# Two query chunks per step in a thresholded attention followed by a gated MLP: score tiles in pairs, one threshold pass of 2304 columns

## The chip, the cores and the metric

The kernel runs on one core of a Trainium2 chip. The metric is the device time of one execution in microseconds, lower is better. Executions of one kernel agree to about 1% here. Each kernel below was profiled once and, beside the kernel before on the same chip, timed in three rounds.

Engine names in the profile: PE is TensorE (matmuls), PEld its weight loads, DVE VectorE, ACT ScalarE, POOL GpSimd, SPq the queue of the sync engine, which issues nearly all transfers here. L490 is line 490 of the kernel that was profiled, so the same instruction has other line numbers in other kernels.

## The reference, cut to what matters

```python
def _attn_ref(q, k, v, tau):                      # 8 batches, 8 heads, 576 queries, 64 wide
    scores = (1.0 / np.sqrt(64)) * np.matmul(q, k.transpose(0, 1, 3, 2))
    thresh = np.max(scores, axis=-1, keepdims=True) - tau
    scores = np.where(scores >= thresh, scores, -1000000000.0)
    scores = scores - np.max(scores, axis=-1, keepdims=True)
    attn = np.exp(scores)
    attn = attn / (np.sum(attn, axis=-1, keepdims=True) + 1e-09)
    return np.matmul(attn, v)

def _moe_ref(x, w_in, w_spatial, b_spatial, w_out):  # x: 8 x 576 x 512, the heads side by side
    h = np.maximum(x @ w_in, 0.0)
    u, v = h[..., :512], h[..., 512:]
    v_n = (v - mean(v)) / np.sqrt(var(v) + 1e-06)    # over the last axis
    v_s = np.einsum('ts,bsd->btd', w_spatial, v_n) + b_spatial[None, :, None]
    return (u * v_s) @ w_out
```

## The kernel before

The 64 heads are worked on in 32 pairs. The work on one pair is called a slot. The 576 queries are four chunks of 128 for each of the two heads, and one chunk (the remainder) that holds the last 64 queries of both. So a slot has five steps, c = 0 to 4. In a step the kernel

1. multiplies queries with keys into one of two score tiles in PSUM (TensorE),
2. takes each row's maximum (VectorE, `negm`),
3. takes the exponential of scores less maximum (ScalarE, `e`),
4. one step later zeroes what lies under exp(-tau): the threshold pass (VectorE, `p`),
5. after every second chunk transposes both chunks' probabilities by a transfer (`pT`); the remainder's are transposed by a transfer of their own (`ptr<-pr`).

A slot later the transposed probabilities are multiplied with the values: `pv` part 0 (chunks 0 and 1) and part 1 (chunks 2, 3 and the remainder). Beside that, up to two jobs fill each step: transpositions of the next pair's queries and keys on TensorE, the parts of `pv`, and one matmul of the gMLP of the batch before. Each job has a matmul and an eviction from one of two small PSUM banks. The step of the kernel before, cut:

```python
def step(i, c, f1, f2):                 # f1, f2: (engine of the eviction, matmul, eviction)
    if i is not None:
        s = scores(i, c)                                        # PE, one of two score tiles
    while held:
        held.pop(0)()                                           # eviction left by the step before
    if f1:
        f1[1]()
        if f1[0] == "act":
            f1[2]()
    ...
    nc.vector.tensor_reduce(out=nm[:, 0:nh], in_=s, axis=AX.X, op=ALU.max, negate=True)
    if f1 and f1[0] == "dve":
        f1[2]()
    ...                                                         # exponentials on ACT
    if unmasked:
        mask()                                                  # pass over the chunk before
    for f in ready:
        f()                                                     # transfers: outputs, xT
    ...
    if f2:
        f2[1]()
        ...                                                     # its eviction, or held

def mask():
    i, c, e = unmasked.pop()
    if c < 4:
        pt = p_ring[c // 2]
        ef = e.rearrange("p h s -> p (h s)")
        nc.vector.scalar_tensor_tensor(out=pt[:, c % 2, :], in0=ef, scalar=ctau, in1=ef,
                                       op0=ALU.is_ge, op1=ALU.mult)
        if c % 2:
            dst = ptp.tile([P, 2, 9, P], BF16, name="pT")
            nc.sync.dma_start_transpose(...)                    # both chunks
    else:
        pts[i, 2] = ptr_ring[i % 3]
        nc.sync.dma_start_transpose(out=pts[i, 2][:, :, 0:P], in_=pr_ring[i % 2])
```

The order of the jobs in a slot: queries' transposition (c = 0), keys' (c = 1), the remainder's of both (c = 2), `pv` part 0 (c = 3), part 1 (c = 4), each with a gMLP job. GpSimd copies the remainder's keys and queries into block diagonals (`kd`, `qd`) that the scores of the next slot need.

Of the kernel before, what the change touches and what calls it, by code (L numbers as in the profile page):

```python
# [8 lines left out]
F32 = mybir.dt.float32  # L9
BF16 = mybir.dt.bfloat16  # L10
AX = mybir.AxisListType
ALU = mybir.AluOpType
ACT = mybir.ActivationFunctionType
# [4 lines left out]
def kernel(  # L18
# [24 lines left out]
    const = ctx.enter_context(tc.tile_pool(name="const", bufs=1))  # L43
    qkn = ctx.enter_context(tc.tile_pool(name="qkn", bufs=2))
    qkT = ctx.enter_context(tc.tile_pool(name="qkT", bufs=2))
    ep = ctx.enter_context(tc.tile_pool(name="ep", bufs=3))
    ptp = ctx.enter_context(tc.tile_pool(name="ptp", bufs=5))
    small = ctx.enter_context(tc.tile_pool(name="small", bufs=6))
    xp = ctx.enter_context(tc.tile_pool(name="xp", bufs=2))
# [79 lines left out]
    def view(t, off, dims):  # L129

        return bass.AP(t.tensor, t.offset + off, [t.ap[0]] + dims)
# [188 lines left out]
    def moe_v(b, c):  # L320
# [8 lines left out]
        def ev():  # L329
# [26 lines left out]
            def rest():  # L356
# [7 lines left out]
                nc.gpsimd.tensor_tensor(out=nm, in0=nmean, in1=rs, op=ALU.mult)  # L364
                nc.gpsimd.tensor_scalar(out=dst, in0=vrel[:n], scalar1=rs[:n], scalar2=nm[:n],
                                        op0=ALU.mult, op1=ALU.add)
            later.append((1, rest))
        return "act", mm, ev

    def moe_u(b, f):  # L370
# [83 lines left out]
    def scores(i, c):  # L454



        s = ps_s.tile([P, 1536], F32, name="s")
        qk = qks[i]

        def mm(h, out, lo, n):
            hs = slice(64 * h, 64 * h + 64)
            m = slice(c * P, (c + 1) * P)
            return nc.tensor.matmul(out=out, lhsT=qk[hs, 0, m], rhs=qk[hs, 1, lo:lo + n],  # L464
                                    start=True, stop=True)
        if c < 4:
            nc.tensor.matmul(out=view(s, 512, [[448, 2], [1, 64]]),  # L467
                             lhsT=qk[:, 0, c * P:(c + 1) * P], rhs=kd_ring[i % 2],
                             start=True, stop=True)
            mm(0, s[:, 0:512], 0, 512)  # L470
            mm(1, s[:, 1024:1536], 0, 512)
            return view(s, 0, [[960, 2], [1, S]])
        for lo, off in ((0, 224), (288, 512)):
            nc.tensor.matmul(out=s[:, off:off + 288], lhsT=qd_ring[i % 2],  # L474
                             rhs=qk[:, 1, lo:lo + 288], start=True, stop=True)
        return s[:, 224:800].rearrange("p (h s) -> p h s", h=1)

    def mask():
        i, c, e = unmasked.pop()
        if c < 4:  # L480
            pt = p_ring[c // 2]
            ef = e.rearrange("p h s -> p (h s)")
            nc.vector.scalar_tensor_tensor(out=pt[:, c % 2, :], in0=ef, scalar=ctau, in1=ef,  # L483
                                           op0=ALU.is_ge, op1=ALU.mult)
            if c % 2:
                dst = ptp.tile([P, 2, 9, P], BF16, name="pT")
                nc.sync.dma_start_transpose(out=dst.rearrange("p c b s -> p (c b) s"),
                                            in_=pt.rearrange("p c s -> p (c s)"))
                pts[i, c // 2] = dst
        else:  # L490
            pts[i, 2] = ptr_ring[i % 3]
            nc.sync.dma_start_transpose(out=pts[i, 2][:, :, 0:P], in_=pr_ring[i % 2])

    def step(i, c, f1, f2):

        if i is not None:
            s = scores(i, c)
        while held:
            held.pop(0)()
        if f1:  # L500
            f1[1]()
            if f1[0] == "act":
                f1[2]()
        if i is not None:
            nh = 2 if c < 4 else 1
            nm = small.tile([P, 2], F32, name="negm")
            nc.vector.tensor_reduce(out=nm[:, 0:nh], in_=s, axis=AX.X, op=ALU.max, negate=True)  # L507
        if f1 and f1[0] == "dve":
            f1[2]()
        due = [f for n, f in later if n <= 0]  # L510
        later[:] = [(n - 1, f) for n, f in later if n > 0]
        if i is not None:
            e = ep.tile([P, 2, S], F32, name="e")
            if c == 4:

                nc.vector.tensor_scalar_add(out=nm[:, 0:1], in0=nm[:, 0:1], scalar1=float(tau))  # L516
                nc.scalar.activation(out=e[:, 0, :], in_=s[:, 0, :], func=ACT.Prelu,  # L517
                                     bias=nm[:, 0:1], alpha=1e30)
                nc.scalar.activation(out=pr_ring[i % 2][:, 0:S], in_=e[:, 0, :], func=ACT.Exp)
            for h in range(2 if c < 4 else 0):  # L520
                nc.scalar.activation(out=e[:, h, :], in_=s[:, h, :], func=ACT.Exp,  # L521
                                     bias=nm[:, h:h + 1])
        ready = sends[:]
        sends.clear()
        if unmasked:
            mask()
        for f in ready:
            f()
        if i is not None:
            unmasked.append((i, c, e))  # L530
        for f in due:
            f()
        if f2:
            f2[1]()
            if f2[0] == "dve":
                f2[2]()
            else:
                held.append(f2[2])


    chores = {13: (load_bias, 0)}
    for n, g0, d, f in ((4, 6, 4, load_w_in), (3, 8, 4, load_ws), (5, 23, 3, shape_ws),
                        (1, 15, 1, shape_bias), (1, 37, 1, place_bias), (2, 42, 5, load_w_o)):
        chores.update({g0 + d * j: (f, j) for j in range(n)})



    LAG = 27
    ORDER = "ovuvvuvuvuuososososs"
    jobs = {}  # L550
    for b in range(B - 1):
# [14 lines left out]
    with tc.manual_schedule():  # L566
# [20 lines left out]
        clear_rest()  # L587
        shape_qk(1)
        queue = []
        for g in range(5 * NPAIR + (len(last) + 1) // 2):  # L590
            slot, c = divmod(g, 5)
            i = slot if slot < NPAIR else None
            if i is not None:
                if c == 2 and slot + 2 < NPAIR:
                    shape_qk(slot + 2)
                if c == 0:
                    shape_v(slot)
                if c == 0 and slot % 2 and slot + 3 < NPAIR or g == 0:
                    for w in range(3):
                        queue.extend(load(slot + (3 if g else 2), 2, w))  # L600
                if g in chores:
                    chores[g][0](chores[g][1])
            else:
                done_with.add("scores")
            fs = []
            if slot + 1 < NPAIR and c < 3:
                fs.append(qk_rem(slot + 1) if c == 2 else qk_main(slot + 1, c))
            if 1 <= slot < NPAIR and c >= 3:
                fs.append(pv(slot - 1, c - 3))
            if g in jobs:  # L610
                fs.append(jobs[g][0](*jobs[g][1:]))
            fs.sort(key=lambda f: f[0])
            if i is None:
                n = 2 * (g - 5 * NPAIR)
                fs = [f(b, j) for f, b, j in last[n:n + 2]]
            for f in queue[:1 if g > 4 else 2]:
                queue.pop(0)()
            step(i, c, fs[0] if fs else None, fs[1] if len(fs) > 1 else None)
        while held:
            held.pop(0)()  # L620
        for f in sends:
# [36 lines left out]
```

## Time and profile before

| | us |
|---|---|
| time, median of 4 runs (with those beside the changed kernel) | 533.2 (530.9 to 534.9) |
| span of the profiled execution | 527.5 |
| start to the end of slot 0 | 24.8 |
| 31 slots after that, mean | 14.94 |
| after the end of the last slot (tail) | 39.6 |

The second exponential of the remainder chunk (`pr`) happens once in each slot, and its start is used as the slot's mark. Lines in order of time have the columns start, duration, engine, line, operation. First the sync queue, then TensorE, in the kernel before, in order of time (columns: start, duration, engine, line, operation):

```profile
256.62 1.24 SPq L492 DMA_TRANSPOSE ptr<-pr  x1
```

```profile
263.88 0.48 PE L281 MATMUL f<-v,ptr 128*128 128x65 bf16 x10
```

The remainder's probabilities are issued to be transposed at 256.62 us and used at 263.88. That is 7.3 us, and landing takes 3.7 us in the median. The kernel before almost never waits for them: 5.3 us in the whole span, in three waits.

### The profile page before, as it was taken

Reading aid. Unit: us, or ns where it says so; the run is one execution under the profiler, and the core shown is the slowest. Engines: PE = TensorE matmul, PEld = TensorE weight load, DVE = VectorE, ACT = ScalarE, POOL = GpSimd, SP = SyncE. Lnnn points to the kernel's source line nnn. Section 1 sums busy time; section 2 is a strip of 40 time slices with the busy share of each in tenths; the row PEclk is TensorE's granted clock in tenths of the full one; section 3 lists DMA queues with packets and bytes.
Section 4 is the critical chain, followed back from the end, with each engine's and each line's share of the span. In section 5 each row is a group of like instructions: output and inputs, shape, how many; then the busy total and the mean of one; then the engine's idle time right before and its main releaser. Section 6 shows DMA issues by size and latency. Waiting matters only on the chain.

```text
span 527.5 us, 9770 instructions
## 1 busy us (share of the span) xinstructions
PE 471.3 (89%) x3560; PEld 256.5 (49%) x3560; DVE 446.4 (85%) x537; ACT 351.0 (67%) x641; POOL 262.3 (50%) x473
## 2 busy tenths in 40 slices
PE   6786877997899999999999999999999999999886
PEld 3343443544455555555454555555455554545433
DVE  2997899898898889899998889998998889989353
ACT  2665566794578866787668875787668875787251
POOL 4625656597615842387405843288405843265020
PEclk9899899999999999999999999999999999999989
DMA  7599997997989997979979886889989796657812
GB/s 231 107 191 202 214 214 137 210 163 155 200 154 212 177 209 163 218 145 200 190 150 212 165 206 153 202 157 194 184 173 220 157 199 152 128 101 135 173 51 89
DMA packets 243599, 90.88 MB, mean 172 GB/s; under 512 B 213024, under 2 KB 238112, under 8 KB 243552
## 3 DMA queue, kind: packets, MB, share of 16 engines
q1 hardware_dynamic: 241936, 88.39, 80.6%
q0 software_dynamic: 1200, 1.58, 2.4%
q8 instruction: 28, 0.46, 0.4%
q10 hardware_dynamic: 416, 0.30, 0.2%
q14 instruction: 19, 0.16, 0.1%
HBM read 33.31 MB, written 9.44 MB: 81 GB/s over the span
## 4 chain that ended last, share of the span: by engine, by line
PE 36%; DVE 27%; DMA 12%; ACT 10%; issue 7%; POOL 4%; SPq 2%; ACTq 0%; POOLq 0%; DVEq 0%
DVE negm L507 12%; DVE p L483 11%; PE s L464 10%; ACT e L521 6%; PE f L281 5%; DMA pT<-p 4%; PE f L407 3%; PE s L474 3%; PE s L467 3%; PE f L326 2%; PE f L230 2%; DMA ptr<-pr 2%; PE f L377 2%; DMA xT<-xn 2%; DVE xn L292 2%
## 5 line engine op out<-in xcount | busy, mean ns | idle before, releaser
L507 DVE TENSOR_REDUCE negm<-s 128x2 f32<-128x1152 f32 (+1 forms) x160 | 196.8, 1232 | 46.2 <-PE s L464 45.2
L521 ACT ACTIVATE e<-s,negm 128x576 f32<-128x576 f32 x256 | 176.0, 740 | 64.4 <-DVE negm L507 53.8
L483 DVE SCALAR_TENSOR_TENSOR p<-e,ctau 128x1152 bf16<-128x1152 f32 x128 | 189.8, 1483 | 2.1 <-DMA pT<-p 1.3
L464 PE MATMUL s<-qkT 64*128 64x512 f32 x512 | 148.6, 658 | 0.0
L253 POOL COPY kd<-qkT 64x64 f32<-64x64 f32 x64 | 18.3, 286 | 101.2 <-ACT qkT L248 99.1
L467 PE MATMUL s<-kd,qkT 128*128 128x128 f32 x256 | 55.2, 298 | 11.5 <-ACT e L521 6.6
L467 PEld LDWEIGHTS s<-kd,qkT 128*128 128x128 f32 x256 | 45.1, 196 | 25.3 <-ACT e L521 7.4
L281 PEld LDWEIGHTS <-pT 128*128 128x128 bf16 x1024 | 41.8, 97 | 15.2 <-issue 12.3
L141 POOL COPY qn<-ql 128x640 f32<-128x640 f32 x32 | 27.2, 851 | 41.6 <-DMA ql<-in_k_dram 25.0
L464 PEld LDWEIGHTS s<-qkT 64*128 64x128 f32 x512 | 39.6, 189 | 15.9 <-issue 1.1
L517 ACT ACTIVATE e<-s,negm 128x576 f32<-128x576 f32 x32 | 23.7, 740 | 33.7 <-DVE negm L516 30.7
L281 PE MATMUL f<-v,pT 128*128 128x65 bf16 x1008 | 45.6, 194 | 0.0
L407 PE MATMUL f<-wsT,vn 128*128 128x512 bf16 x150 | 37.5, 379 | 6.6 <-DMA wsT<-parts 3.4
L474 PE MATMUL s<-qkT,qd 128*128 128x288 f32 x128 | 38.4, 423 | 4.5 <-issue 2.4
L326 PE MATMUL f<-w_in,xT 128*128 128x512 bf16 x140 | 36.6, 380 | 2.5 <-ACT vrel L351 1.3
L256 POOL TENSOR_SCALAR qd<-qkT 64x64 f32<-64x64 f32 x64 | 35.9, 562 | 4.6
L274 PE MATMUL f<-v,pT 128*128 128x130 bf16 x126 | 27.6, 219 | 9.6 <-ACT uT L394 3.2
L436 PE MATMUL f<-w_o,gT 128*128 128x512 bf16 (+1 forms) x128 | 33.9, 388 | 2.0 <-DVE gT L424 2.0
L235 ACT ACTIVATE qkT<-f 128x512 f32<-128x512 f32 x32 | 19.0, 595 | 23.5 <-PE f L230 22.9
L363 POOL TENSOR_TENSOR rs<-rs,mhalf 128x1 f32<-128x1 f32 x35 | 33.2, 948 | 2.9
L292 DVE TENSOR_TENSOR xn<-f,r 128x256 bf16<-128x256 f32 (+1 forms) x63 | 30.9, 490 | 2.2
L377 PE MATMUL f<-xT,w_in 128*128 128x512 bf16 x120 | 30.8, 378 | 1.6 <-ACT vrel L351 0.9
(105 smaller groups left out, 622.0 us busy)
## 6 DMA issues: line engine op xcount, KB each, us to landing
vl<-in_v_dram SPq DMA_DIRECT2D x16, 512.0 KB, 5.0
out_dram<-o SPq DMA_DIRECT2D x32, 256.0 KB, 2.7
ql<-in_q_dram SPq DMA_DIRECT2D x15, 512.0 KB, 4.4
kl<-in_k_dram SPq DMA_DIRECT2D x15, 512.0 KB, 4.8
uT<-in_moe_w_spatial_dram SPq DMA_DIRECT2D x2, 576.0 KB, 6.1
vl<-in_v_dram SPq DMA_DIRECT2D x16, 64.0 KB, 3.0
pT<-p SPq DMA_TRANSPOSE x64, 5.7
w_in<-in_moe_w_in_dram POOLq DMA_DIRECT2D x4, 256.0 KB, 7.2
```

The source lines that it names most:

```text
L256: nc.gpsimd.tensor_scalar(out=qd[hs, hs], in0=qks[i][hs, 0, 512:576], scalar1=scale, scalar2=0.0, op0=ALU.mult, op1=ALU.add)
L281: nc.tensor.matmul(out=t[:, at + 65 * h:at + 65 * h + 65], lhsT=lhs, rhs=vt[:, 6 * h + j, :], start=(c == 4 and j == 0), stop=(h == 1 and ...
L292: nc.vector.tensor_tensor(out=xn[:, c0:c1, :].rearrange("p c (h d) -> p (c h) d", h=2), in0=o[:, :, 0:64], in1=r[:, 0:w].unsqueeze(2).broa ...
L326: nc.tensor.matmul(out=t, lhsT=xts[b][:, f, c * P:(c + 1) * P], rhs=w_in[:, f, 512:1024], start=(f == 0), stop=(f == 3))
L377: nc.tensor.matmul(out=t, lhsT=w_in[:, m, f * P:(f + 1) * P], rhs=xts[b][:, m, 0:512], start=(m == 0), stop=(m == 3))
L407: nc.tensor.matmul(out=t, lhsT=vn[:, c, f * P:(f + 1) * P], rhs=wsT[:, c, 0:512], start=(c == 0), stop=(c == 4))
L464: return nc.tensor.matmul(out=out, lhsT=qk[hs, 0, m], rhs=qk[hs, 1, lo:lo + n], start=True, stop=True)
L467: nc.tensor.matmul(out=view(s, 512, [[448, 2], [1, 64]]), lhsT=qk[:, 0, c * P:(c + 1) * P], rhs=kd_ring[i % 2], start=True, stop=True)
L474: nc.tensor.matmul(out=s[:, off:off + 288], lhsT=qd_ring[i % 2], rhs=qk[:, 1, lo:lo + 288], start=True, stop=True)
L483: nc.vector.scalar_tensor_tensor(out=pt[:, c % 2, :], in0=ef, scalar=ctau, in1=ef, op0=ALU.is_ge, op1=ALU.mult)
L507: nc.vector.tensor_reduce(out=nm[:, 0:nh], in_=s, axis=AX.X, op=ALU.max, negate=True)
L521: nc.scalar.activation(out=e[:, h, :], in_=s[:, h, :], func=ACT.Exp, bias=nm[:, h:h + 1])
```

## The change

The intent: join two chunks in one unit, so that TensorE makes two score tiles back to back, VectorE makes one pass of 2304 columns in place of two of 1152, and four jobs lie beside it; the remainder is a unit with two jobs. Attention times values comes earlier in the slot, so the gMLP of a batch can follow two steps sooner and two of its jobs leave the tail. The core of the diff:

```diff
+        ts.append(ps_s.tile([P, 1536], F32, name="s"))
+        if c < 4:
+            rest(c)
+            mains(c)
+            ts.append(ps_s.tile([P, 1536], F32, name="s"))
+            mains(c + 1)
+            rest(c + 1)
...
     def mask():
         i, c, e = unmasked.pop()
         if c < 4:
-            pt = p_ring[c // 2]
-            ef = e.rearrange("p h s -> p (h s)")
-            nc.vector.scalar_tensor_tensor(out=pt[:, c % 2, :], in0=ef, scalar=ctau, in1=ef,
-                                           op0=ALU.is_ge, op1=ALU.mult)
-            if c % 2:
+            pt = p_ring[c // 2].rearrange("p c s -> p (c s)")
+            nc.vector.scalar_tensor_tensor(out=pt, in0=e, scalar=ctau, in1=e, op0=ALU.is_ge,
+                                           op1=ALU.mult)
...
+    def unit(i, c, fs):
+        n = 2 if c < 4 else 1
+        ss = scores(i, c)
+        while held:
+            held.pop(0)()
...
+        for k, s in enumerate(ss):
+            f = fs[2 * k]
+            if f:
+                f[1]()
+                if f[0] == "act" and k == 0:
+                    f[2]()
+            nm = small.tile([P, 2], F32, name="negm")
+            nc.vector.tensor_reduce(out=nm[:, 0:s.shape[1]], in_=s, axis=AX.X, op=ALU.max,
+                                    negate=True)
+            if f and f[0] == "dve" and k == 0:
+                f[2]()
+            if k == 1 and fs[1]:
+                fs[1][2]()
...                                     # exponentials; the remainder's two
+            if k == n - 1 and unmasked:
+                mask()                  # of the unit before
...
+            f = fs[2 * k + 1]
+            if f:
+                f[1]()
+                if k == n - 1:
+                    held.append(f[2])
+        for f in ready + due:
+            f()
...
-    LAG = 27
+    LAG = 25
...
+            for c, ks in ((0, (0, 1)), (2, (2, 3)), (4, (4,))):
...
+                unit(slot, c, {0: lambda: qk(qk_main, 0) + val(0) + qk(qk_main, 1) + job(0),
+                               2: lambda: qk(qk_rem) + val(1) + job(1) + job(2),
+                               4: lambda: job(3) + job(4)}[c]())
```

## The prediction

> **What bounds the kernel now.** I read the page's totals first, then busy time by stretch, then the waits, then the two engines in order of time. A slot below is the work on one pair of heads: five steps in the kernel before, three units in the changed one. The end of each slot shows in the trace as the start of the second exponential of its remainder chunk (pr, L519), 32 of them.
>
> The page's totals, then its two largest VectorE groups:
>
> ```profile
> PE 471.3 (89%) x3560; PEld 256.5 (49%) x3560; DVE 446.4 (85%) x537; ACT 351.0 (67%) x641; POOL 262.3 (50%) x473
> ...
> L507 DVE TENSOR_REDUCE negm<-s 128x2 f32<-128x1152 f32 (+1 forms) x160 | 196.8, 1232 | 46.2 <-PE s L464 45.2
> ...
> L483 DVE SCALAR_TENSOR_TENSOR p<-e,ctau 128x1152 bf16<-128x1152 f32 x128 | 189.8, 1483 | 2.1 <-DMA pT<-p 1.3
> ```
>
> No engine is full over the whole span. The marks of pr at 205.24, 219.50, 234.37, 249.57 and 264.93 us give slots of 14.26, 14.87, 15.20 and 15.36 us, and from 205.24 to 444.56 us the mean of 16 slots is 14.96. Busy time slot by slot in that stretch (columns: window, length, then PE, PEld, DVE, ACT, POOL busy, clock, DMA share):
>
> ```profile
> 205.24:219.50 14.26, 13.94 (x122) 7.82 (x120) 13.47 (x17) 10.03 (x17) 1.98 (x5) 1.00 0.89 190
> 219.50:234.37 14.87, 14.03 (x105) 7.61 (x105) 13.18 (x15) 12.96 (x28) 11.33 (x20) 1.00 0.77 172
> 234.37:249.57 15.20, 14.37 (x119) 8.06 (x120) 13.36 (x17) 11.45 (x22) 12.53 (x23) 1.00 0.94 176
> 249.57:264.93 15.36, 14.55 (x107) 7.95 (x105) 14.08 (x16) 9.79 (x16) 5.42 (x10) 1.00 0.93 193
> ```
>
> TensorE is busy 14.2 us of 14.96 and VectorE 13.5. They are bound to each other: VectorE is idle about 1.45 us a slot, and 19.7 us of that over the 16 slots is the row maximum waiting for scores. TensorE's busy time includes pipelined tails. From start to start the work of a slot is about 13.7 us. So both have over a microsecond of slack, and what sets the slot is who waits for whom.
>
> The lengths I need are distances from one start to the next, because instructions overlap at their ends. VectorE in order of time:
>
> ```profile
> 243.79 1.34 DVE L507 TENSOR_REDUCE negm<-s 128x2 f32<-128x1152 f32 x1
> 245.06 1.40 DVE L483 SCALAR_TENSOR_TENSOR p<-e,ctau 128x1152 bf16<-128x1152 f32 x1
> 246.38 0.17 DVE L291 RECIPROCAL r<-f 128x4 f32<-128x4 f32 x1
> 246.59 0.42 DVE L292 TENSOR_TENSOR xn<-f,r 128x256 bf16<-128x256 f32 x1
> ...
> 263.13 0.74 DVE L507 TENSOR_REDUCE negm<-s 128x1 f32<-128x576 f32 x1
> 263.91 0.15 DVE L516 TENSOR_SCALAR negm<-negm 128x1 f32<-128x1 f32 x1
> 263.98 1.41 DVE L483 SCALAR_TENSOR_TENSOR p<-e,ctau 128x1152 bf16<-128x1152 f32 x1
> 265.31 0.19 DVE L291 RECIPROCAL r<-f 128x6 f32<-128x6 f32 x1
> 265.53 0.56 DVE L292 TENSOR_TENSOR xn<-f,r 128x384 bf16<-128x384 f32 x1
> 266.01 1.34 DVE L507 TENSOR_REDUCE negm<-s 128x2 f32<-128x1152 f32 x1
> ```
>
> A maximum over two heads takes 1.27 us (243.79 to 245.06), a threshold pass 1.32 (245.06 to 246.38), eviction of the first part of attention times values 0.63 (0.21 and 0.42), of the second 0.70 (265.31 to 266.01), the remainder's maximum with its addition 0.85 (263.13 to 263.98). TensorE, an output job, then one chunk of scores, then the next job:
>
> ```profile
> 250.72 1.02 PE L436 MATMUL f<-w_o,gT 128*128 128x512 bf16 x4
> 251.58 0.39 PE L467 MATMUL s<-kd,qkT 128*128 128x128 f32 x2
> 251.90 1.13 PE L464 MATMUL s<-qkT 64*128 64x512 f32 x4
> 252.96 0.66 PE L230 MATMUL f<-identf,kn 128*128 128x128 f32 x4
> ```
>
> A job takes 0.86 us and a chunk of scores 1.38.
>
> [...]
>
> **The change, part by part.**
>
> *The pass of 2304 columns* replaces two. [...]
>
> *Both score tiles at once.* The score pool has two tiles and both now belong to one unit. VectorE's order over a slot is read from the program: maxima 0 and 1, eviction of part 0, maxima 2 and 3, eviction of part 1, pass over chunks 0 and 1, remainder maximum, pass over chunks 2 and 3. TensorE's order is scores 0 and 1, transpose, part 0, transpose, job, scores 2 and 3, and so on. The job in the first unit uses the small bank that part 0 used (two such banks in turn). It waits for part 0's eviction, which stands on VectorE behind maximum 1, and scores 2 stand on TensorE behind that job. This closes a ring from the last pass of one slot to that of the next:
>
> last pass 2.52 + maxima 0 and 1 2.54 + eviction 0.63 + job 0.76 + scores 2 and 3 2.76 + maximum 3 1.27 + eviction 0.70 + first pass 2.52 + remainder 0.85 = 14.55 us.
>
> (0.76 is the mean of three jobs of 0.86 and the short one of 0.46.) Four crossings between engines at 0.05 make it 14.75. The spatial jobs' products also stand in this VectorE order: four of 0.60 and one of 0.33 in four slots, 0.68 a slot. The ring is 15.4 us, 0.47 above 14.96. Seen otherwise: VectorE works 13.5 - 0.24 = 13.3 us a slot and stands idle while the job and scores 2 run, about 2.2 us where it now idles 1.45.
>
> To this I add 0.14 for longer passes (they average 1.445 in this stretch against the median of 1.409; four a slot), 0.1 for the slot where a spatial job waits for another's eviction behind the long pass, and 0.1 to 0.2 for transfers. Together some 0.8 us a slot, over the 27 slots from the first gMLP job on: +21 us.
>
> *Part 0 comes sooner.* Its transposed probabilities were written about six steps, 18 us, before use. Now they leave after the first pass, which ends some 0.8 us before the last pass starts, and are needed 4.5 us after that start if part 0 is not to delay its eviction. That leaves 5.3 us; landing takes 4.7 to 5.5 us in the median in the steady stretches, 7.7 at most, and 8.2 in the median between 20 and 80 us. In the five slots before gMLP work the ring has no job: scores 2 wait for the exponentials of chunk 0 instead, and it is about 13.4 us, below the 14.4 that those slots now take. Late landings may take it to 15 or 16. I allow +3 us for the five.
>
> *gMLP two steps closer* moves two jobs, an output and a spatial one, from the tail into the loop. At 0.86 and 1.08 us on TensorE the tail loses 2 us. The new buffers themselves cost nothing.
>
> Sum: 533.5 + 21 + 3 - 2 = 555.5; I say 554.
>
> **The rivals.** First, TensorE becomes the only bound: scores back to back never wait, and the slot falls to the 13.7 us of its work plus small waits, say 14.5. For it speaks TensorE's 95% in the steady slots; against it, the bank between part 0 and the job. It would give 533 - 12 - 2, about 519. Second, the passes saved and the waits gained cancel: if several links overlap more than I count, the slot stays near 15.0 and the time near 532. Third, transfers rule: part 0, or the remainder's transpose queued behind the last long transpose and the sequence's loads, arrives late each slot. For it speak the DMA share of 0.77 to 0.94 and 5.7 us to landing; each microsecond late adds up to 27, so 565 to 580. Fourth, ScalarE in the two slots full of first-layer jobs: by the same durations it needs some 14.9 us in one of them, but 12.1 on average, so it adds little.
>
> **Range and chances.** The ring alone, with nothing added, gives 27 x 0.47 = 13 us, less 2 for the tail: 544. Landing stalls of half a microsecond a slot lead to 568. With room for a link that I misread, the range is 536 to 571. Faster by over 2% needs the ring to be broken somewhere: 0.07. Within 2% (up to 544): 0.18. Slower: 0.75.
>
> **What would show it.** Right: steady slots of 15.3 to 16 us; VectorE's wait for scores at the third chunk's maximum of 1.5 us or more in every slot; TensorE waiting on VectorE's xn ahead of the first unit's job; long passes of 2.6 us when alone; TensorE's busy share lower in the steady stretch; a tail about 2 us shorter. Wrong: slots under 15 us, with the job not waiting for the eviction; or the largest TensorE wait being for pT or ptr, which would make transfers the cause.

The pass of 2304 columns came to 2.52 us from start to start, 0.12 less than two of 1.32, so 0.24 us a slot and at most 7.7 us over 64 passes. Both long passes in the ring's 14.55 us, the 0.24 in VectorE's work and the 0.12 and 7.7 us in the expectations below come from it; the sum stood at 555.5, given as 554. The trace of kernel 3 later shows 2.52 us for the pass (304.33 to 306.85). The ring takes it that VectorE works in the program's order; in the trace each of its lines starts about as the one before it ends (243.79 + 1.34 = 245.13 against 245.06). The 0.05 us for a crossing between engines is an estimate; in the critical chain of the kernel before, 0.04 us lie between VectorE's `gT` and the output job at 212.10.

## The result

The changed kernel takes 644.9 us in the median of 4 runs (638.5 to 648.1). The ratio is 1.208 (95% interval 1.198 to 1.219). Executions over 1.5% slower than the fastest of the same kernel are left out of the means. Here and below a ratio is the mean time of one kernel's runs over that of the kernel before in the same rounds, so it is not quite the ratio of the medians. The direction was as predicted, the size was not: +112 us against +21, and above the stated range of 536 to 571.

| profiled execution | before | changed |
|---|---|---|
| span | 527.5 | 643.8 |
| to the end of slot 0 | 24.8 | 25.1 |
| 31 slots after that, mean | 14.94 | 18.59 |
| tail | 39.6 | 42.4 |

All of it is in the slots: 31 x 3.65 = 113 us, of which 50 are in the first 12, 61 in the next 16 and 2 in the last 3. The totals and the chain that ended last, changed kernel:

```profile
PE 487.1 (76%) x3511; PEld 273.8 (43%) x3560; DVE 431.5 (67%) x473; ACT 343.5 (53%) x641; POOL 264.8 (41%) x473
...
PE 36%; DVE 24%; DMA 19%; ACT 12%; issue 4%; SPq 3%; POOL 1%; ACTq 0%; POOLq 0%
DMA ptr<-pr 17%; DVE p L490 14%; PE s L470 9%; ACT e L529 8%; DVE negm L519 8%; PE s L482 4%; PE f L327 4%; PE f L408 4%; PE f L378 3%; PE s L463 3%; PE f L437 3%; PE f L282 3%; DMA out_dram<-o 1%; PE f L231 1%; ACT sq L360 1%
```

No engine is near full any more, and one transfer, the remainder's transpose, is the largest single part of the chain. Busy time in 16 steady slots (window, length, then PE, PEld, DVE, ACT, POOL busy, granted clock, DMA share, GB/s), before, then changed:

```profile
205.24:444.56 239.32, 227.54 (x1778) 125.65 (x1776) 216.39 (x245) 176.72 (x329) 122.99 (x228) 1.00 0.87 182
```

```profile
255.28:555.78 300.50, 237.31 (x1748) 134.48 (x1776) 209.09 (x213) 172.97 (x328) 123.05 (x228) 0.93 0.71 145
```

VectorE's work fell, from 216.4/16 = 13.5 us a slot to 209.1/16 = 13.1, but its idle time rose from 22.9/16 = 1.4 to 91.4/16 = 5.7. TensorE's clock was granted at 1.00 before and 0.93 now. The waits of the changed kernel (engine, line, for whom: us in total, times, longest):

```profile
DVE r L292 <- PE f L282: 89.1, 32, 7.1
DVE negm L519 <- PE s L470: 78.2, 34, 7.0
...
PE f L282 <- DMA ptr<-pr: 71.5, 30, 5.6
...
PE f L275 <- DMA pT<-p: 22.7, 19, 3.9
```

TensorE stood 71.5 us waiting for the remainder's transposed probabilities, in 30 of 32 slots, and 22.7 us for the others. VectorE's 89.1 us ahead of `r` is the same wait passed on: `r` is the first instruction of the eviction of part 1. How it comes about is on the sync queue, changed kernel:

```profile
407.14 2.68 SPq L493 DMA_TRANSPOSE pT<-p  x1
409.87 1.28 SPq L300 DMA_TRANSPOSE xT<-xn  x1
411.25 0.55 SPq L448 DMA_DIRECT2D out_dram<-o  x1
411.89 0.53 SPq L114 DMA_DIRECT2D ql<-in_q_dram  x1
412.47 0.63 SPq L121 DMA_DIRECT2D ql<-in_q_dram  x1
413.19 1.25 SPq L497 DMA_TRANSPOSE ptr<-pr  x1
```

and on ScalarE and TensorE:

```profile
405.44 0.68 ACT L536 ACTIVATE pr<-er 128x576 bf16<-128x576 f32 x1
```

```profile
414.45 0.41 PE L282 MATMUL f<-v,pT 128*128 128x65 bf16 x8
417.12 0.49 PE L282 MATMUL f<-v,ptr 128*128 128x65 bf16 x10 [2.25 <-DMA ptr<-pr]
```

`pr` was ready at 406.1 us. Its transpose was issued at 413.2, behind the long transpose of chunks 2 and 3, the transpose of `xn`, an output and two loads, each of which takes the queue 0.5 to 2.7 us; and the long transpose could itself be issued only when its pass ended, at 407.1. In this record each transfer is issued about as the one before leaves the queue (407.14 + 2.68 = 409.82 against 409.87, and so on), so `ptr` waited there 7.1 us; then it took 3.9 us to land. In the kernel before the wait in the queue was nearly as long (`pr` ready at 250.25, its transpose issued at 256.62, 6.4 us); but there the use stood in the fifth step of the next slot, and now it stands in the second unit. The chain of the changed kernel shows that this closes a ring (start, us, what):

```profile
413.19 3.87 DMA ptr<-pr
...
417.12 0.50 PE f L282 x10
...
417.64 0.21 DVE r L292
...
418.35 2.61 DVE p L490
420.95 0.68 DVE negm L519
...
421.74 2.62 DVE p L490
```

The late part 1 delays its eviction, behind it in VectorE's order stands the first long pass, behind that the remainder's maximum and the second long pass, and behind that on the sync queue the next `ptr`.

The changed kernel has a check of this in itself. In its last three slots no load is left in the queue: `ptr` is issued 5.1 to 5.9 us after `pr` is ready, TensorE waits for it 0.9 us in all, the clock is 1.00, and the slots are 15.1, 15.4 and 15.1 us. That is 0.8 us a slot over the same three slots of the kernel before.

### The profile page after: what moved, and what is told of

Its sections match the earlier page's. It is cut to its first block, busy times and chain, and to the rows that moved or that the text cites. A ratio compares the mean times of both kernels' runs of the same rounds, so it can differ in the third digit from the quotient of the medians.

```text
span 643.8 us, 9547 instructions
## 1 busy us (share of the span) xinstructions
PE 487.1 (76%) x3511; PEld 273.8 (43%) x3560; DVE 431.5 (67%) x473; ACT 343.5 (53%) x641; POOL 264.8 (41%) x473
## 4 chain that ended last, share of the span: by engine, by line
PE 36%; DVE 24%; DMA 19%; ACT 12%; issue 4%; SPq 3%; POOL 1%; ACTq 0%; POOLq 0%
DMA ptr<-pr 17%; DVE p L490 14%; PE s L470 9%; ACT e L529 8%; DVE negm L519 8%; PE s L482 4%; PE f L327 4%; PE f L408 4%; PE f L378 3%; PE s L463 3%; PE f L437 3%; PE f L282 3%; DMA out_dram<-o 1%; PE f L231 1%; ACT sq L360 1%
## 5 line engine op out<-in xcount | busy, mean ns | idle before, releaser
L529 ACT ACTIVATE e<-s,negm 128x576 f32<-128x576 f32 x256 | 168.6, 746 | 7.9 <-DVE negm L519 7.9
L490 DVE SCALAR_TENSOR_TENSOR p<-e,ctau 128x2304 bf16<-128x2304 f32 x64 | 169.1, 2642 | 0.3 <-issue 0.3
L470 PE MATMUL s<-qkT 64*128 64x512 f32 x512 | 133.6, 635 | 6.2 <-ACT er L534 5.9
L254 POOL COPY kd<-qkT 64x64 f32<-64x64 f32 x64 | 17.2, 269 | 189.2 <-ACT qkT L249 187.3
L282 PE MATMUL f<-v,ptr 128*128 128x65 bf16 x310 | 17.9, 212 | 71.5 <-DMA ptr<-pr 71.5
L292 DVE RECIPROCAL r<-f 128x4 f32<-128x4 f32 (+1 forms) x63 | 11.7, 185 | 89.1 <-PE f L282 89.1
L354 POOL TENSOR_SCALAR nmean<-sm 128x1 f32<-128x1 f32 x35 | 43.7, 1250 | 60.8 <-ACT vrel L352 60.6
L470 PEld LDWEIGHTS s<-qkT 64*128 64x128 f32 x512 | 43.9, 192 | 50.6 <-ACT er L534 18.9
L534 ACT ACTIVATE er<-s,negm 128x576 f32<-128x576 f32 x32 | 23.6, 738 | 63.5 <-DVE negm L533 63.5
L437 PE MATMUL f<-w_o,gT 128*128 128x512 bf16 (+1 forms) x114 | 36.8, 416 | 17.3 <-DVE xn L293 15.6
L142 POOL COPY qn<-ql 128x640 f32<-128x640 f32 x32 | 35.5, 1108 | 30.2 <-DMA ql<-in_k_dram 13.1
L352 ACT ACTIVATE vrel<-f 128x512 f32<-128x512 f32 x35 | 20.8, 594 | 50.1 <-PE f L327 50.1
L275 PE MATMUL f<-v,pT 128*128 128x130 bf16 x126 | 27.8, 221 | 24.7 <-DMA pT<-p 22.7
L282 PEld LDWEIGHTS <-ptr 128*128 128x128 bf16 x320 | 14.3, 110 | 75.2 <-DMA ptr<-pr 75.2
L445 ACT COPY o<-f 128x512 f32<-128x512 f32 (+1 forms) x31 | 18.4, 594 | 48.9 <-PE f L437 48.0
```

The source lines that it names most:

```text
L142: nc.gpsimd.tensor_copy(out=t, in_=ld_ring[i // 2 % 2][w][:, 2 * (i % 2):2 * (i % 2) + 2].rearrange("p h c d -> p c h d"))
L275: nc.tensor.matmul(out=t[:, at:at + 130], lhsT=pt[:, 4, :], rhs=vt[:, 4:6, :].rearrange("p b d -> p (b d)"), start=True, stop=False)
L282: nc.tensor.matmul(out=t[:, at + 65 * h:at + 65 * h + 65], lhsT=lhs, rhs=vt[:, 6 * h + j, :], start=(c == 4 and j == 0), stop=(h == 1 and ...
L354: nc.gpsimd.tensor_scalar(out=nmean, in0=sm, scalar1=-1.0 / 512, scalar2=0.0, op0=ALU.mult, op1=ALU.add)
L437: nc.tensor.matmul(out=t[:n], lhsT=gs[b][:, f, c * P:c * P + n], rhs=w_o[:, f, :], start=(f == 0), stop=(f == 3))
L470: nc.tensor.matmul(out=ts[-1][:, 1024 * h:1024 * h + 512], lhsT=qk[hs, 0, c * P:(c + 1) * P], rhs=qk[hs, 1, 0:512], start=True, stop=True)
```

## The experiments

All kernels gave the right result. Each block shows the edit against the kernel named, cut, then what was on record before it ran. A steady slot is the mean of the same 16 slots in each kernel. The profiles of kernels 8 and 11 are of slow runs.

**1. The remainder's transpose early.** Against the changed kernel:

```diff
                 nc.scalar.activation(out=pr_ring[i % 2][:, 0:S], in_=e, func=ACT.Exp)
+                pts[i, 2] = ptr_ring[i % 3]
+                nc.sync.dma_start_transpose(out=pts[i, 2][:, :, 0:P], in_=pr_ring[i % 2])
...
-        else:
-            pts[i, 2] = ptr_ring[i % 3]
-            nc.sync.dma_start_transpose(out=pts[i, 2][:, :, 0:P], in_=pr_ring[i % 2])
```

> The changed kernel, with the transpose of the remainder's probabilities issued in the remainder's own unit, ahead of the long transpose of chunks 2 and 3, instead of in the next unit behind that transpose, the output's and the loads. Theory T (the slots of 18.6 us are set by the remainder's probabilities landing late; TensorE waited 71.5 us for them): those waits fall under 10 us, the granted clock comes back above 0.96, slots fall to 15.4 to 16.2 us (the ring through the small bank that the prediction worked out, with nothing late), time 550 to 570. Rival R (the ring alone makes the slots, the late landing only fills time that TensorE would lose anyway): the waits move to the eviction of part 0 and the time stays above 625. Rival C (the lower clock is the cause and not a result): clock and time stay as they are.

Measured: 583.1 us (576.8 to 585.8), ratio 1.095 (1.087 to 1.102). One transfer issued at another place takes 62 of the 112 us away. The waits for `ptr` are gone and the clock is at 0.953. It is slower than theory T said, 583 against 550 to 570, with steady slots of 16.4 us; in them the clock is 0.97. What is left are waits for the other transpose; from this kernel's waits:

```profile
PE f L275 <- DMA pT<-p: 42.1, 28, 5.9
```

So rivals R and C fail as the main cause, and half of the loss is still to explain.

**2. The same, with evictions ahead of the second maximum.** Against kernel 1:

```diff
+            if k == 1 and fs[1]:
+                fs[1][2]()
             nm = small.tile([P, 2], F32, name="negm")
             nc.vector.tensor_reduce(out=nm[:, 0:s.shape[1]], in_=s, axis=AX.X, op=ALU.max,
                                     negate=True)
...
-            if k == 1 and fs[1]:
-                fs[1][2]()
```

> As the run before, and the eviction of part 0 (and of part 1) stands on VectorE ahead of the second maximum of its unit, not behind it. If the ring through the small bank is what bounds the slot once the remainder lands early, one maximum of 1.27 us leaves it: slots 0.6 to 1.2 us shorter than in the run before, 18 to 37 us in all. If the landing of the long transpose of chunks 0 and 1 bounds it, VectorE now waits for part 0 ahead of the maximum, and the time is within 1% of the run before or above it.

Measured: 615.3 us, ratio 1.160 (1.155 to 1.166): 5.5% over kernel 1. The eviction now waits in VectorE's order for a matmul that waits for a transfer, and the maximum stands behind it. This kernel's waits show it: the wait ahead of the evictions is larger than in kernel 1 (32.6 us), and ScalarE waits for maxima.

```profile
ACT e L525 <- DVE negm L518: 105.3, 77, 4.9
DVE r L292 <- PE f L282: 102.1, 53, 5.7
```

The change's own place for the eviction is the better one. The run does not tell how strong the ring through the small bank is, since it put a worse wait in its place.

**3. The long pass alone, in the kernel before.** One pass for two chunks, in the later of the two steps:

```diff
-            pt = p_ring[c // 2]
-            ef = e.rearrange("p h s -> p (h s)")
-            nc.vector.scalar_tensor_tensor(out=pt[:, c % 2, :], in0=ef, scalar=ctau, in1=ef,
-                                           op0=ALU.is_ge, op1=ALU.mult)
             if c % 2:
+                pt = p_ring[c // 2]
+                nc.vector.scalar_tensor_tensor(out=pt.rearrange("p c s -> p (c s)"), in0=e,
+                                               scalar=ctau, in1=e, op0=ALU.is_ge, op1=ALU.mult)
```

> The kernel before with one thing changed: one threshold pass of 2304 columns for each two chunks, in the step where the second of the two passes stood, so that the transposes start where they started. Prediction's term: 0.12 us a pass, 7.7 us at most, if all of it were on the path: 525 to 533. Theory that the pass's length costs more than it saves, since a pass of 2.6 us stands between two maxima and scores wait for both: a slot of 15.2 to 15.6 us, 540 to 553.

Measured: 558.1 us, ratio 1.051 (1.047 to 1.055), steady slots 15.87 against 14.96. The pass that saves VectorE work costs 26 us in the old schedule. VectorE in order of time in this kernel:

```profile
299.82 1.36 DVE L508 TENSOR_REDUCE negm<-s 128x2 f32<-128x1152 f32 x1 [1.16 <-PE s L466]
303.05 1.36 DVE L508 TENSOR_REDUCE negm<-s 128x2 f32<-128x1152 f32 x1 [1.87 <-PE s L466]
304.33 2.61 DVE L485 SCALAR_TENSOR_TENSOR p<-e,ctau 128x2304 bf16<-128x2304 f32 x1
306.85 1.35 DVE L508 TENSOR_REDUCE negm<-s 128x2 f32<-128x1152 f32 x1
```

The edit also puts `e` of two chunks in one larger buffer, two of these in place of three small ones (cut here); in this kernel's waits ScalarE never waits for a pass to free one. In the steps without a pass VectorE waits for scores (1.16 and 1.87 us), and in the step with it the next maximum comes 2.5 us late. ScalarE's wait for maxima rose from 53.8 to 108.3 us.

**4. Attention times values later in the slot.** Against the changed kernel, with the remainder's transpose left where the change put it:

```diff
-    LAG = 25
+    LAG = 27
...
-                unit(slot, c, {0: lambda: qk(qk_main, 0) + val(0) + qk(qk_main, 1) + job(0),
-                               2: lambda: qk(qk_rem) + val(1) + job(1) + job(2),
-                               4: lambda: job(3) + job(4)}[c]())
+                unit(slot, c, {0: lambda: qk(qk_main, 0) + job(0) + qk(qk_main, 1) + job(1),
+                               2: lambda: qk(qk_rem) + val(0) + job(2) + job(3),
+                               4: lambda: val(1) + job(4)}[c]())
```

> The changed kernel with attention times values moved back to where it stood before (part 0 in the second unit, part 1 in the third, the gMLP jobs taking their places, gMLP two steps later again); the remainder's transpose stays where the change put it. Theory T: distance is as good as an earlier issue, so waits for pT and ptr go (from 102 us on TensorE to under 15), slots 14.6 to 15.6 us, time 530 to 550. Rival R: the job in the first unit no longer waits for part 0 here, so the ring is opened as well and this run alone does not tell T from R; with the first run it does. If the time stays above 600, the two tiles at once are the cause.

Measured: 579.4 us, ratio 1.093 (1.087 to 1.098). Distance is as good as an earlier issue: TensorE's waits for `pT` and `ptr` fall to 4.5 and 2.3 us. But the slots are 16.8 us, not 14.6 to 15.6. They come in four kinds in turn, of about 15.0, 15.3, 18.9 and 17.2, so something other than landing costs the latter two.

**5 and 6. Two passes of 1152 in the place of one long one.** Kernel 5 is kernel 1, kernel 6 is kernel 3, each with

```diff
-            nc.vector.scalar_tensor_tensor(out=pt, in0=e, scalar=ctau, in1=e, op0=ALU.is_ge,
-                                           op1=ALU.mult)
+            for lo in (0, 1152):
+                nc.vector.scalar_tensor_tensor(out=pt[:, lo:lo + 1152], in0=e[:, lo:lo + 1152],
+                                               scalar=ctau, in1=e[:, lo:lo + 1152],
+                                               op0=ALU.is_ge, op1=ALU.mult)
```

> The changed kernel with the remainder's transpose early, and each pass of 2304 columns replaced by two of 1152 at the same place in the same order. By the prediction's arithmetic the halves cost 0.12 us a pair more: 64 x 0.12 = 7.7 us, 591 against 583. Theory L (a long pass shuts GpSimd out for its whole length of 2.6 us, and what GpSimd then delivers late holds ScalarE and TensorE up): GpSimd's longest single instructions fall from 2.6 to about 1.4 us and the time falls below 575.

> The kernel before with both passes of a pair of chunks kept at their length of 1152 columns but moved together into the later step, where the run with long passes had its pass of 2304. That run took 558 against 532. Theory B (bunching: two passes' worth between two maxima in one step and none in the other): 556 to 562, as with the long pass. Theory L (the length of a single instruction[...]): under 540.

Measured: kernel 5 589.9 us, ratio 1.108 (1.101 to 1.115), 7 us over kernel 1. Kernel 6 563.1 us, ratio 1.056 (1.050 to 1.062), 5 us over kernel 3 (3 by the ratios). The intervals of each pair overlap, so the times agree with the prediction's 7.7 us no more than in sign. The traces show the saving itself: from the start of a long pass to the next start there are 2.52 us (304.33 to 306.85 above), from the start of two halves 2.66 (308.33 to 310.99 in kernel 6), so 0.14 us a pass. And in kernel 3 it was not the length that cost 26 us: two short passes moved together cost 30. It is the bunching, two passes' worth of work between two maxima and none between the next two. Theory L came true in its first half only. In the traces of the kernels before and changed GpSimd's longest copy of the key diagonal takes 1.37 us where passes have 1152 columns and 2.61 where they have 2304. In kernel 5 the mean copy takes 0.47 us against 0.52 in kernel 1, but the time did not fall.

**7 and 8. The first pass in VectorE's gap.** Kernel 7 is kernel 1 with the pass over chunks 0 and 1 ahead of the maximum of chunk 2; kernel 8 the same in halves.

```diff
+            if c == 2 and k == 0 and unmasked:
+                mask()
             nm = small.tile([P, 2], F32, name="negm")
```

> The changed kernel with the remainder's transpose early, and the pass over chunks 0 and 1 moved ahead of the maximum of chunk 2, into the time in which VectorE waits for scores 2. The ring theory: 2.5 us of pass leave the ring, and the transposed probabilities leave some 4 us sooner, so waits for pT go from 42 us to under 10; the slot is then held by the work of VectorE and TensorE: 14.3 to 15.6 us, time 515 to 550. If the slots stay above 16 us, neither the ring nor the landing of pT was what made them.

> The run before this with each long pass in two halves of 1152. By the prediction's arithmetic 7.7 us longer at most than with long passes; by theory L shorter by more than 5 us.

Measured: kernel 7 576.9 us, ratio 1.081 (1.075 to 1.086), steady slots 16.3. Kernel 8 561.4 us in the median, but one run of four at 551.1, at a clock of 0.972 against 0.956 to 0.959; the other three count as slow runs, so it has no ratio. Even its slow runs lie below all of kernel 7. Kernel 7 misses its expectation. Its waits show why halves help here though they cost in 5 and 6:

```profile
DVE p L490 <- ACT e L528: 35.5, 31, 2.7
```

A long pass can only start when the exponentials of both chunks are there. Put early, it waits 1.1 us a slot for the second. The first half needs only the first chunk, and kernel 8 has next to no such wait (1.7 us in all). Theory L had also forecast this gain; but ScalarE waited only 4.4 us for GpSimd's row means in kernel 7, so its share is small at most.

**9 and 10. Part 0 behind the job of the first unit**, in kernel 1 and in kernel 8:

```diff
-                unit(slot, c, {0: lambda: qk(qk_main, 0) + val(0) + qk(qk_main, 1) + job(0),
+                unit(slot, c, {0: lambda: qk(qk_main, 0) + job(0) + qk(qk_main, 1) + val(0),
```

> The changed kernel with the remainder's transpose early (583 us, slots 16.4), and in the first unit the gMLP job and part 0 of attention times values change places: the job no longer waits for part 0's eviction, and scores 2 wait for no work of VectorE on a small bank. This opens the ring of the prediction and gives pT 1.4 us more. If the ring bounds the slot: slots 15.2 to 15.8, time 550 to 570, TensorE's wait for xn ahead of the job gone (18 + 23 us). If the landing of pT bounds it, the wait for pT falls by up to 1.4 us a slot from 42 us, with much the same time; the wait lines tell the two apart: waits for pT still over 15 us, or not. If neither counts (something else, as GpSimd's products): 578 to 588.

> The run with the pass in the gap and in halves (561 us, slots 15.5), with the same change of places. There VectorE has the pass to do while TensorE works off the job and scores 2, so the ring should be slack already: ring theory says 552 to 565, no more than 1.5% either way. A gain above 2% would mean that the ring still held there.

Measured: kernel 9 588.0 us, ratio 1.102 (1.094 to 1.109), no better than kernel 1. The job's wait for `xn` is gone (18.0 us in kernel 1, under 2 for each job now), but waits for `pT` are still 30.8 us, and VectorE's wait ahead of `r` rose from 32.6 to 75.9. The ring was opened and the eviction, now first in the next unit, waits for part 0 instead. Kernel 10: 595.6 us, ratio 1.114 (1.106 to 1.122), a clear miss. There the eviction stands ahead of the pass that should fill the gap, and holds it up:

```profile
407.20 0.18 DVE L292 RECIPROCAL r<-f 128x4 f32<-128x4 f32 x1 [1.57 <-PE f L282]
407.42 0.42 DVE L293 TENSOR_TENSOR xn<-f,r 128x256 bf16<-128x256 f32 x1
407.76 2.74 DVE L491 SCALAR_TENSOR_TENSOR p<-e,ctau 128x1152 bf16<-128x1152 f32 x2
```

**11. The remainder's scores sooner.** Kernel 8 with one job moved from the second unit to the third:

```diff
-                               2: lambda: qk(qk_rem) + val(1) + job(1) + job(2),
-                               4: lambda: job(3) + job(4)}[c]())
+                               2: lambda: qk(qk_rem) + val(1) + job(1),
+                               4: lambda: job(2) + job(3) + job(4)}[c]())
...                                     # and in the unit, a third job after the second
+        for f in fs[2 * n:]:
+            if f:
+                while held:
+                    held.pop(0)()
+                f[1]()
+                held.append(f[2])
```

> The run with the pass in the gap and in halves, with one job moved from behind part 1 to behind the remainder's scores, which so come 0.9 us sooner. There the one long wait that VectorE has left is for these scores, 46.6 us in 32 slots. If that wait is what keeps it above the kernel before, 0.5 to 0.9 us a slot: 535 to 547. If TensorE's work only moves elsewhere: 555 to 565.

Measured: 545.4 us in the median; the ratio is 1.013 (1.002 to 1.025). The wait for these scores fell from 46.6 to 24.2 us. Its steady slots are 14.44, 14.30, 16.30 and 14.82 us in turn: 14.97 in the mean, as in the kernel before. Three kinds are below that mean. In the long one TensorE waits for GpSimd, kernel 11:

```profile
366.56 2.75 DVE L491 SCALAR_TENSOR_TENSOR p<-e,ctau 128x1152 bf16<-128x1152 f32 x2
366.64 2.76 POOL L254 COPY kd<-qkT 64x64 f32<-64x64 f32 x2
...
369.46 0.49 PE L463 MATMUL s<-kd,qkT 128*128 128x128 f32 x2 [1.22 <-POOL kd L254]
```

Two copies of 64x64 that take 0.23 us each in the median of the kernels before and changed last 2.76 us here, as long as the two passes beside them, and end 0.09 us after the second. So in halves, too, the two copies in a row lasted until both passes had ended.

**12. The changed order with nothing late.** So far each run that took the late landing away changed the order on an engine too. Here the changed kernel keeps its order, but attention times values works on the pair before the last:

```diff
-                return [pv(slot - 1, part)] if slot else [None]
+                return [pv(slot - 2, part)] if slot > 1 else [None]
...
-    LAG = 25
+    LAG = 30
...
-    last += [(pv, NPAIR - 1, h) for h in range(2)]
+    last += [(pv, n, h) for n in (NPAIR - 2, NPAIR - 1) for h in range(2)]
```

> The changed kernel with nothing moved on any engine inside a slot, but attention times values working on the pair of heads before the last one, so that both kinds of transposed probabilities have a whole slot more to land (gMLP five steps later to match, so the tail is some 7 us longer). Waits of TensorE for pT and ptr: from 94 us to under 10. Ring of the prediction: steady slots of 15.2 to 15.8 us in the mean, against 18.8. Time 545 to 565. A mean under 15.0 would refute the ring as a bound; a mean over 16.2 would say that a third cause of its size is at work, which the waits must then name.

Measured: 577.0 us, ratio 1.084 (1.078 to 1.090). TensorE waits for neither kind of probabilities any more, and the tail is 8 us longer, as reckoned. The 31 slots take 500.0 us in all, against 576.3 in the changed kernel and 463.1 in the kernel before: 76 of the slots' 113 us are gone, 37 are left. Up to 8 of the 76 are work that now stands in the tail. In the 16 steady slots, where the work is the same, late landing cost 18.78 - 16.61 = 2.2 us a slot of 3.8. The mean steady slot is 16.6, over the expected 15.2 to 15.8, but it is a mean of unlike slots: by the first four of the steady stretch 16.7, 16.9, 15.0 and 17.3 us, later 16.7, 15.1, 15.0 and 18.9 to 20.1. The two short kinds are near the prediction's ring of 15.4. In the longest, kernel 12 (the lines of VectorE, GpSimd and TensorE that matter):

```profile
326.40 2.75 DVE L490 SCALAR_TENSOR_TENSOR p<-e,ctau 128x2304 bf16<-128x2304 f32 x1
...
326.70 2.85 POOL L254 COPY kd<-qkT 64x64 f32<-64x64 f32 x2
...
329.60 0.79 PE L463 MATMUL s<-kd,qkT 128*128 128x128 f32 x2 [3.07 <-POOL kd L254]
...
330.32 3.79 PE L470 MATMUL s<-qkT 64*128 64x512 f32 x8
```

The two copies of the key diagonal take 2.85 us beside a pass of 2.75 and end 0.4 us after it, TensorE stands 3.07 us, and then the eight matmuls of two chunks take 3.79 us where they take 1.99 at 338.05. TensorE's other work is drawn out as well until about 335.5 us: the two matmuls at 329.60 and at 334.04 take 0.79 us against 0.49 at 337.63, a transposition 1.06 (334.62) against 0.66 (336.37). The mean granted clock of the steady slots was 0.96; what lowers it, no run shows.

**13. The key diagonal sooner, in kernel 11**, and **14. the same in kernel 12**: the remainder's transposition changes places with the keys'.

```diff
-                unit(slot, c, {0: lambda: qk(qk_main, 0) + val(0) + qk(qk_main, 1) + job(0),
-                               2: lambda: qk(qk_rem) + val(1) + ...
+                unit(slot, c, {0: lambda: qk(qk_main, 0) + val(0) + qk(qk_rem) + job(0),
+                               2: lambda: qk(qk_main, 1) + val(1) + ...
```

> The last variant (545 us) with the remainder's transposition of the next pair one unit sooner, changing places with the transposition of its keys, so that GpSimd's copies of the key diagonal are not caught by the pass at the end of the slot. If those copies hold the slot that is still 16.3 us long (TensorE waited 1.2 us for them there), it falls to about 14.6 and the time by 7 to 13 us, to 532 to 538: level with the kernel before. If the slot stays above 16, the cause is another.

> The run with values one slot later (577 us, slots of 15.1, 15.0, 16.7 and 19 to 20 us in turn), with the remainder's transposition one unit sooner, so that GpSimd copies the key diagonal well before the long passes. If those copies make the long fourth slot: it falls to 14.6 to 15.8 us, the mean from 16.6 to 15.2 to 15.8, which is the prediction's ring (15.4) and what it added for the slot with two spatial jobs in a row; time 545 to 558. If the fourth slot stays above 17 us, the cause is another GpSimd product or ScalarE's wait for one.

Measured: kernel 13 538.8 us (537.3 to 541.7), ratio 1.014 (1.009 to 1.019). The long slot fell from 16.30 to about 15.25, the wait for `kd` to one wait of 1.1 us, but two other kinds grew, to 14.8 and 15.0; against kernel 11 nothing is gained for certain. It is the best variant found, and still a little slower than the kernel before (by less than 2%, but clear of the noise). That loss isn't in its steady slots, which at 14.86 us are no longer than those before: to the end of slot 0 it takes 27.4 us and for the next 12 slots 190.3, against 24.8 and 180.5. No run looked into these. Kernel 14: 573.0 us, ratio 1.074 (1.065 to 1.083), less gained than expected, and its interval overlaps with that of kernel 12. The longest kind fell from 19 to 20 us to 16.0, and TensorE's waits for `kd` from 21.4 us in eight waits to one of 1.1, so the copies did make it. But two others are now at 15.3 or 17.0 and at 16.6 or 18.2 from one batch to the next, and the mean is 16.2. The two lengths go with the clock (0.90 or 0.91 in the longer ones, 1.00 in the others). Two slots of one kind in kernel 14 (columns as above):

```profile
215.54:232.13 16.59, 14.59 (x123) 8.25 (x123) 14.09 (x16) 8.97 (x15) 3.07 (x8) 1.00 0.96 201
```

```profile
279.94:298.17 18.23, 16.06 (x123) 9.00 (x123) 14.09 (x16) 8.98 (x15) 3.07 (x8) 0.91 0.87 180
```

In the second of them the prediction's ring can be seen at work, with the lower clock (0.91) on top:

```profile
284.93 0.42 DVE L293 TENSOR_TENSOR xn<-f,r 128x256 bf16<-128x256 f32 x1
285.41 0.44 PE L437 MATMUL f<-w_o,gT 128*128 128x512 bf16 x1 [1.82 <-DVE xn L293]
...
287.48 2.73 PE L470 MATMUL s<-qkT 64*128 64x512 f32 x8
...
289.41 2.62 DVE L519 TENSOR_REDUCE negm<-s 128x2 f32<-128x1152 f32 x2 [4.06 <-PE s L470]
```

The job waits 1.82 us for the eviction of part 0 and VectorE waits 4.06 us for scores 2, whose eight matmuls take 2.73 us. Where they take 1.99 (kernel 12, from 338.05), the second wait is 2.15 us; the prediction had about 2.2. In the shortest kind of slot (249.11 to 263.96, 14.85 us), at a clock of 1.00, VectorE is busy 12.31 us and so stands about 2.5 in all.

| kernel | us | ratio | steady slot |
|---|---|---|---|
| before | 533.2 | 1 | 14.96 |
| changed | 644.9 | 1.208 | 18.78 |
| 1 remainder's transpose early | 583.1 | 1.095 | 16.38 |
| 2 and evictions first | 615.3 | 1.160 | 17.47 |
| 3 before, long pass | 558.1 | 1.051 | 15.87 |
| 4 values later in the slot | 579.4 | 1.093 | 16.83 |
| 5 as 1, two passes | 589.9 | 1.108 | 16.55 |
| 6 before, two passes together | 563.1 | 1.056 | 16.03 |
| 7 as 1, first pass in the gap | 576.9 | 1.081 | 16.32 |
| 8 as 7, in halves | 561.4 | none | 15.51 |
| 9 as 1, part 0 after the job | 588.0 | 1.102 | 16.44 |
| 10 as 8, part 0 after the job | 595.6 | 1.114 | 17.02 |
| 11 as 8, scores 4 sooner | 545.4 | 1.013 | 14.97 |
| 12 values one slot later | 577.0 | 1.084 | 16.61 |
| 13 as 11, diagonal sooner | 538.8 | 1.014 | 14.86 |
| 14 as 12, diagonal sooner | 573.0 | 1.074 | 16.20 |

## Why the prediction was right or wrong

**Right: slower, because waits replace the pass that is saved.** The first rival, that scores back to back make TensorE the only bound, is refuted: TensorE's busy share fell to 76%.

**Right: the saving of the pass.** Predicted 0.12 us a pass; the traces of kernels 3 and 6 show 0.14. The difference in time, 7 us (kernels 1 and 5) and 3 to 5 (kernels 3 and 6), has the right sign and lies within the noise. The long pass is 2.61 to 2.63 us alone, as predicted.

**Right as a mechanism, and near in size where it can be seen: the ring through the small bank.** Predicted 15.4 us a slot, longer with two spatial jobs in a row. With nothing late and the clock at 1.00, the four kinds of slot in kernel 14 take 14.85, 15.34, 15.98 and, in the kind with two spatial jobs in a row, 16.59: a mean of 15.7 (16.2 with the slots at a lower clock). The changed kernel's own last three slots, 15.1 to 15.4 us, fit as well. But the run that opened the ring (kernel 9) gained nothing, as other waits stood ready. So it is shown that the slots have about the ring's length when nothing is late, and not that opening it would help.

**Wrong: the term for transfers, the step that failed.** The prediction added "0.1 to 0.2 for transfers" to each slot, and 3 us in all for the early ones. Kernel 12 measures 2.2 us a steady slot, and 68 to 76 us in all, as some work went to the tail; moving one transpose (kernel 1) alone gives back 62. The third rival had named just this, the remainder's transpose "queued behind the last long transpose and the sequence's loads", and put it at 565 to 580 by counting about a microsecond. It was mis-sized because the margin was worked out for part 0's transpose alone, from time to landing. The remainder's transpose spends nearly twice as long in the queue ahead of its issue as in landing: 7.1 and 3.9 us in the slot shown. The margin of the long transposes was too thin as well: with `ptr` early, TensorE still waits 42.1 us for `pT`, 12.1 of it in the 16 steady slots (kernel 1). The profile before had the numbers: `ptr` issued at 256.62 us and used 7.3 us later, which the change was to shorten by about a third of a slot. And the late landing was taken as a delay added to each slot. In fact it closes a second ring, from the second pass through the sync queue to part 1 and back to the passes.

**Wrong by leaving it out: GpSimd.** The prediction counted the long passes as VectorE's work only. But in the traces of the kernels before and changed 98 instructions or groups of GpSimd begin more than 0.05 us into a threshold pass, and every one ends after that pass, by 0.04 us or more. In kernel 12 this meets the copies of the key diagonal (2.85 us for two), which costs the longest kind of slot 3 to 4 us, as kernel 14 shows by taking it away. Taking it away gained only about 4 us of time, though, as two other kinds of slot then ran at a lower clock (0.90 or 0.91) in some batches. In the changed kernel itself the same shows in GpSimd's mean over the row (`nmean`): it takes 1.25 us on average where it took 0.33, and each of the 24 that last over 0.5 us ends about 0.05 us after a long pass. What TensorE and ScalarE waited for GpSimd there is little (4.1 us for `kd`, 2.5 for `nmean`); its share of the 112 us is not settled apart from the rest.

**Left out as well: the clock.** In the steady slots TensorE was granted a clock of 0.93 in the changed kernel against 1.00 before, and the same work kept it busy 237.3 us against 227.5. The lower clock goes with the waits: in kernel 1, where those for `ptr` are gone, it was 0.97 and TensorE busy 228.4 us. What lowers it no run shows, nor what it adds to each cause above.

**Wrong in sign: the tail.** Predicted 2 us shorter with two jobs less. It is 2.8 us longer (42.4 against 39.6). In its first 8 us the last long transposes, `xT` and `ptr` follow each other on the sync queue; this was not tested by a run.

**Of the signs named ahead:** a wait of VectorE at the third chunk's maximum in every slot, TensorE waiting for `xn` ahead of the first unit's job, and long passes of 2.6 us came true. "The largest TensorE wait being for pT or ptr, which would make transfers the cause" is what happened.

What stays open: the 37 us that the slots of kernel 12 cost above those before are ring, GpSimd and clock together, and no run separates the three shares cleanly. Kernels 3 and 6 show that bunching the passes costs 26 to 30 us in the old order, which may be the same loss seen from another side.

## What to carry to other kernels

Before a consumer is moved closer to its producer, add up everything that a queue issues between the two, not only the time to landing (here 7.1 us in the queue and 3.9 to landing), and check whether the consumer's delay feeds the producer's next turn: then it is a ring and the whole length counts, not the overshoot. Work that fills gaps was worth more here in small pieces spread between the waits than bunched: the length saved 0.14 us a pass, 9 us in all, and the place lost some 30. And GpSimd's work that fell into a long threshold pass of VectorE ended after it here (two copies of 0.23 us took 2.85 beside a pass of 2.75), so see what GpSimd owes to whom in that time.
